# Backward attention loop: score and dP tiles cut into single PSUM banks, exp and product per head, dQ grouped by head and query-tile parity, and a new order of work inside a four-step block

## The chip, the cores and the metric

One Trainium2 chip, one of its cores. The metric is device time in microseconds (us) of one execution. The kernel before takes 1579.33 us (median of three runs, 1575.57 to 1579.68).

Engines: PE (matmuls), PEld (PE's weight loads), DVE (VectorE), ACT (ScalarE), POOL (GpSimd), SP (the engine that issues nearly all DMA here).

## The reference

A transformer block with attention and a gated feed-forward network in parallel, and all its gradients. S = 2048 tokens, D = 448, 16 heads of 28, F = 1792, bf16 in and out.

```python
def _A_ref(x, wqkv, wo):
    q, k, v = split_heads(x @ wqkv)                       # cut: reshape and transpose
    p = _softmax(jnp.einsum("bhqd,bhkd->bhqk", q, k) * (Dh ** -0.5), axis=-1)
    return merge_heads(jnp.einsum("bhqk,bhkd->bhqd", p, v)) @ wo

def _B_ref(x, w_gate, w_up, w_down):
    return (_silu(x @ w_gate) * (x @ w_up)) @ w_down

xn = _layernorm(x)
out = x + _A_ref(xn, wqkv, wo) + _B_ref(xn, w_gate, w_up, w_down)
# reference(...) returns out and, by jax.vjp, the gradients of x, wqkv, wo, w_gate, w_up, w_down
```

## The kernel before

The first 678 us are the forward pass and the parts of the backward pass that don't need attention's gradient. The last 57 us are a tail. Between them lies the backward attention loop, the only part that changes. It runs 512 **steps**; one step is one pair of heads, 128 queries and 512 keys. Four steps are a **block** (512 queries). In a step, PE recomputes the scores (S) of both heads, and dP for the step before. ACT takes exp(S). DVE multiplies dP by that exp, which gives dS. PE then multiplies exp and dS into the accumulators of dV and dK ("kv"). For dQ, dS has to be transposed: SP issues DMA transposes for most query tiles, and PE transposes the rest itself ("T", the `tr_unit`). Once per block PE computes dQ.

Between those, PE gets **fillers**: matmuls of other outputs, which use a PSUM bank called `genb`. They are y (the forward output), dx, dc, dwq (the gradient of wqkv), and "dsp", the transposes that dwq needs. 

A PSUM bank holds 512 fp32 per partition, and there are eight. (The Trainium skill, "PSUM — Partial Sum Buffer", "PSUM: the matmul accumulator" and "The four PSUM rules", says that there are 8 banks of 2 KiB and that one matmul's output lies in one; the allocation here agrees, since both kernels use exactly eight.) Before, they are: `sb` (scores) one tile of two banks, `db` (dP, and also the T tile) two tiles of two banks, `acc` one, `genb` one.

```python
def row(k):                                    # PE: S of step k, dP of step k-1
    if k < NB:
        ...
        s_ps = ps_b.tile([P, 2, 512], FP32, name="sb")             # two banks, one buffer
        for j in range(2):                                          # the two heads
            r = HP * (2 * hp + j)
            PE.matmul(s_ps[:, j, :], lhsT=qside[g, qc][r:r + HP, 0, qi * P:(qi + 1) * P],
                      rhs=kside[g, kc][r:r + HP, 0, :], start=True, stop=True, tile_position=(r, 0))
        sps[k] = s_ps
    if 1 <= k <= NB:
        d_ps = ps_b.tile([P, 2, 512], FP32, name="db", bufs=2)     # 2 x two banks
        ...                                                         # two matmuls, as above

def ew(k):                                     # ACT and DVE
    if k < NB:
        est[k] = bk.tile([P, 2, 512], BF16, name="e_sb", bufs=4)
        ACTE.activation(out=est[k][:], in_=sps.pop(k)[:], func=ACT.Exp, scale=SCALE)
    if 1 <= k <= NB:
        ...
        DVE.tensor_tensor(out=ds[:, qi % 2], in0=dps.pop(k - 1)[:], in1=est[k - 1][:], op=ALU.mult)
        ...                                                         # DMA transposes at qi 1 and 2

def tr_unit(b):                                # T: PE transposes of the last query tile(s)
    ...
    ps = ps_b.tile([P, 8 * (2 - q0), P], BF16, name="db", bufs=2)
    ...                                                             # 8 (16 for b < TB) PE.transpose
    DVE.tensor_copy(out=dsT[b][:, 2 + q0:4]..., in_=ps[:])

def kv(k):                                     # dV and dK, accumulated over 16 steps
    ...
    if last:
        ...
        ACTE.activation(out=dkv[g, hp][:, kc * 512:(kc + 1) * 512], in_=a[:], func=ACT.Copy, ...)

def dq_unit(b):
    ps = ps_b.tile([P, 512], FP32, name="genb")
    ...                                                             # 8 matmuls of 512 columns
    ACTE.mul(out=st[:], in_=ps[:], mul=SCALE)
    POOL.tensor_tensor(out=dq_acc[:, qsl], in0=dq_acc[:, qsl], in1=st[:], op=ALU.add)
    if kc == 3:
        POOL.dma_start(out=mv_[r0:r0 + 64, :], in_=dq_acc[64 - r0:128 - r0, qsl])
        ...                                                         # later: add the two halves

ROOM = {2: 600, 3: 400, 0: 1100}               # ns of filler after step 2, 3 and 0 of a block
for k in range(NB + 12):
    m = k % 4
    row(k); ew(k); ...
    while kv_n < NB and (kv_n <= k - 2 if m % 2 else kv_n <= k - 3 and blk < 1500):
        kv(kv_n); kv_n += 1
    ...                                        # m == 1: dq_unit; m == 2: tr_unit; 2, 3, 0: fill_step(m)
```

The softmax here doesn't subtract the row's maximum and nothing guards it: scores larger than these inputs give would overflow.

Of the kernel before, what the change touches and what calls it, by code (L numbers as in the profile page):

```python
# [16 lines left out]
S = 2048  # L17
# [73 lines left out]
def kernel(  # L91
# [610 lines left out]
    stream, later = [], []  # L702
# [14 lines left out]
    def row(k):  # L717

        if k < NB:
            g, hp, kc, qc, qi = steps[k]  # L720
            have(("q", g, qc), ("k", g, kc))
            s_ps = ps_b.tile([P, 2, 512], FP32, name="sb")
            for j in range(2):
                r = HP * (2 * hp + j)
                PE.matmul(s_ps[:, j, :], lhsT=qside[g, qc][r:r + HP, 0, qi * P:(qi + 1) * P],  # L725
                          rhs=kside[g, kc][r:r + HP, 0, :], start=True, stop=True, tile_position=(r, 0))
            sps[k] = s_ps
        if 1 <= k <= NB:
            g, hp, kc, qc, qi = steps[k - 1]
            d_ps = ps_b.tile([P, 2, 512], FP32, name="db", bufs=2)  # L730
            for j in range(2):
                r = HP * pv(2 * hp + j)
                PE.matmul(d_ps[:, j, :], lhsT=qside[g, qc][r:r + HP, 1, qi * P:(qi + 1) * P],  # L733
                          rhs=kside[g, kc][r:r + HP, 1, :], start=True, stop=True, tile_position=(r, 0))
            dps[k - 1] = d_ps

    def ew(k):
        if k < NB:
            est[k] = bk.tile([P, 2, 512], BF16, name="e_sb", bufs=4)
            ACTE.activation(out=est[k][:], in_=sps.pop(k)[:], func=ACT.Exp, scale=SCALE)  # L740
        if 1 <= k <= NB:
# [5 lines left out]
            DVE.tensor_tensor(out=ds[:, qi % 2], in0=dps.pop(k - 1)[:], in1=est[k - 1][:], op=ALU.mult)  # L747


# [8 lines left out]
    def tr_unit(b):  # L758
        ds = dss.pop(4 * b + 3)
        q0 = 1 if b >= TB else 0  # L760
        ps = ps_b.tile([P, 8 * (2 - q0), P], BF16, name="db", bufs=2)
        for c in range(8 * (2 - q0)):
            PE.transpose(ps[:, c, :], ds[:, q0 + c // 8, c // 4 % 2, (c % 4) * P:(c % 4 + 1) * P], ident_bf[:])  # L763
        DVE.tensor_copy(out=dsT[b][:, 2 + q0:4].rearrange("p q j kt s -> p (q j kt) s"), in_=ps[:])  # L764
# [35 lines left out]
    def dq_unit(b):  # L800

        while later:
            later.pop(0)()
# [4 lines left out]
        for kk in range(2):  # L808
            for par in range(2):
                for j in range(2):  # L810
                    r = HP * (2 * par + j)
                    h = HP * (2 * hp + j)
                    kt = 2 * kk + par
                    PE.matmul(ps[r:r + HP, :], lhsT=ks[:, kt, h:h + HP], rhs=t[:, :, j, kt, :],  # L814
                              start=(kk == 0), stop=(kk == 1), tile_position=(0, r), skip_group_check=True)
        qsl = slice(qc * 512, (qc + 1) * 512)
        if kc == 0:
            ACTE.mul(out=dq_acc[:, qsl], in_=ps[:], mul=SCALE)
            return
# [9 lines left out]
        ACTE.mul(out=st[:], in_=ps[:], mul=SCALE)  # L829
        POOL.tensor_tensor(out=dq_acc[:, qsl], in0=dq_acc[:, qsl], in1=st[:], op=ALU.add)  # L830
        if kc == 3:
            if hp == 0 and qc == 0:
                dqT[g] = bk.tile([P, S], BF16, name="dqT", bufs=1)
            r0 = 64 * hp
            mv_ = bk.tile([P, 512], FP32, name="dq_mv", bufs=1)
            POOL.dma_start(out=mv_[r0:r0 + 64, :], in_=dq_acc[64 - r0:128 - r0, qsl])

            def merge():
                POOL.tensor_tensor(out=dqT[g][r0:r0 + 64, qsl], in0=dq_acc[r0:r0 + 64, qsl],
                                   in1=mv_[r0:r0 + 64, :], op=ALU.add)  # L840
                if hp == 1 and g < G - 1:
                    store(dqkvT_d[3 * g, :, qsl], dqT[g][:, qsl])
                if hp == 1 and qc == 3 and g < G - 1:

                    stream[3:3] = [(480, lambda t8=t8: dsp_unit(g, 0, t8)) for t8 in range(2)]

                    at = [i for i, u in enumerate(stream) if u[1] in (dx_open, tail_open)]
                    at = max(at[0] + 1, 5) if g != 1 else 5
                    stream[at:at] = [(2590, lambda c=c: dwq_unit(g, c)) for c in range(4)]
            later.append(merge)  # L850
# [4 lines left out]
    def dsp_unit(g, kind, t8, tag="genb"):  # L855
        if g not in dsp:
            dsp[g] = bk.tile([P, NT, 3, P], BF16, name="dsp", bufs=1)
        src = dqT[g] if kind == 0 else dkv[g, kind - 1]
        ps = ps_b.tile([P, 8, P], BF16, name=tag, bufs=2 if tag == "rest" else 1)
        for j in range(8):  # L860
            t = 8 * t8 + j
            PE.transpose(ps[:, j, :], src[:, t * P:(t + 1) * P], ident_bf[:])
            if j < 7:
                yield 60
        DVE.tensor_copy(out=dsp[g][:, 8 * t8:8 * t8 + 8, kind, :], in_=ps[:])
        s_done.add((g, kind, t8))
        yield 60
# [3 lines left out]
    def dwq_unit(g, c, tag="genb"):  # L871
        d0, dn = DCH[c]
        ps = ps_b.tile([P, 3 * P], FP32, name=tag, bufs=2 if tag == "rest" else 1)
        for t in range(NT):
            PE.matmul(ps[:dn, :], lhsT=xn_sp[:, t, d0:d0 + dn], rhs=dsp[g][:, t].rearrange("p k r -> p (k r)"),  # L875
                      start=(t == 0), stop=(t == NT - 1))
            if t < NT - 1:
# [8 lines left out]
              o[:dn].rearrange("p k h r -> p k (h r)"))  # L886
        yield 162
# [66 lines left out]
    def dx_open():  # L954
        yst.close()
# [99 lines left out]
    ROOM = {2: 600, 3: 400, 0: 1100}  # L1055
    DRIP = 175 << 10
    cur, blk = None, 0

    def need(done):
        while not done():  # L1060
            for _ in stream.pop(0)[1]():
                pass

    def fill_step(m):
        nonlocal cur, blk
        room = ROOM[m]
        rest = sum(ROOM[x] for x in {2: (2, 3, 0), 3: (3, 0), 0: (0,)}[m]) + 150
        if cur is None:
            while stream and stream[0][0] == 0:
                for _ in stream.pop(0)[1]():  # L1070
                    pass
            if not stream or (m != 2 and stream[0][0] > rest):
                return
            ns, u = stream.pop(0)
            cur = u()
            blk += ns
        for ns in cur:
            room -= ns
            if room < ns / 2 and m != 0:
                return  # L1080
        cur = None

    kv_n = 0
    for k in range(NB + 12):
        now = k
        if k < NB:
# [5 lines left out]
            if hp == 1 and g + 1 < G and qi == 2 and (kc, qc) in ((1, 0), (3, 1), (3, 2), (3, 3)):  # L1092
# [8 lines left out]

        while kv_n < NB and (kv_n <= k - 2 if m % 2 else kv_n <= k - 3 and blk < 1500):
            kv(kv_n)
            kv_n += 1
        if m == 0 and 36 <= k < NB:
            fill_step(0)
        if m == 1:
# [3 lines left out]
        elif m == 2:  # L1111
            b = (k - 6) // 4
            if 0 <= b < NB // 4:
                tr_unit(b)
            blk = 0
            if 36 <= k < NB:
                fill_step(2)
        elif m == 3 and 36 <= k < NB:
            fill_step(3)
# [45 lines left out]
    def dx_b(t):  # L1165
# [7 lines left out]
        t2 = bk.tile([P, 512], FP32, name="e_sb", bufs=4)[:, :D]  # L1173
# [9 lines left out]
    def dsq_unit(t4, tag):  # L1183
# [9 lines left out]
    rest += [dsq_unit(t4, "rest") for t4 in range(4)]  # L1193
# [45 lines left out]
```

## Time and profile before

| window (us) | what | length |
|---|---|---|
| 0–678 | forward and early backward | 678 |
| 678–1516 | backward attention loop, 512 steps | 838 (1.636 a step) |
| 1516–1573 | tail | 57 |

Two stretches of the loop, from the windows view of the kernel before: busy time (and number of instructions) of each engine, then the granted PE clock, the DMA share and GB/s.

```profile
core 0: us, PE busy (x) PEld busy (x) DVE busy (x) ACT busy (x) POOL busy (x), PEclk, DMA share, GB/s
678.00:750.00 72.00, 48.80 (x505) 20.65 (x505) 55.15 (x48) 44.77 (x49) 3.80 (x3) 0.77 0.74 158
750.00:1516.00 766.00, 695.37 (x6899) 285.74 (x6895) 694.64 (x720) 563.31 (x655) 150.16 (x133) 0.99 1.00 196
```

PE and DVE are busy for 91% of the second stretch, ACT for 74%. The costliest groups of the loop (page, part 5: busy us and mean ns of one, then the idle time before them and what ended most of it):

```profile
L740 ACT ACTIVATE e_sb<-sb 128x1024 bf16<-128x1024 f32 x512 | 523.9, 1023 | 222.7 <-PE db L733 158.0
L747 DVE TENSOR_TENSOR ds_sb<-db,e_sb 128x1024 bf16<-128x1024 f32 x512 | 623.7, 1222 | 80.8 <-PE db L733 52.6
...
L764 DVE COPY dsT<-db 128x1024 bf16<-128x1024 bf16 (+1 forms) x128 | 91.5, 715 | 0.8 <-PE db L763 0.8
```

The timeline of ACT in the kernel before (start, length, what, and in brackets the idle time before it and its releaser):

```profile
1197.80 1.02 ACT L740 ACTIVATE e_sb<-sb 128x1024 bf16<-128x1024 f32 x1 [0.52 <-PE db L733]
1199.30 1.02 ACT L740 ACTIVATE e_sb<-sb 128x1024 bf16<-128x1024 f32 x1 [0.48 <-PE db L733]
1200.44 0.60 ACT L829 ACTIVATE dq_st<-genb 128x512 f32<-128x512 f32 x1
1200.93 1.02 ACT L740 ACTIVATE e_sb<-sb 128x1024 bf16<-128x1024 f32 x1
1202.43 1.02 ACT L740 ACTIVATE e_sb<-sb 128x1024 bf16<-128x1024 f32 x1 [0.48 <-PE sb L725]
```

Exps follow at 1.50 us although one takes 1.02: the only scores tile is free when an exp ends, and the next exp waits 0.48 us for new scores. The waits view shows the sum of this, and the waits of POOL for the small dQ transfer:

```profile
ACT e_sb L740 <- PE db L733: 158.0, 270, 5.5
...
POOL dqT L839 <- DMA dq_mv<-dq_acc: 94.8, 24, 8.0
...
ACT e_sb L740 <- PE sb L725: 62.5, 90, 17.8
```

### The profile page before, as it was taken

Reading aid. Unit: us, or ns where it says so; the run is one execution under the profiler, and the core shown is the slowest. Engines: PE = TensorE matmul, PEld = TensorE weight load, DVE = VectorE, ACT = ScalarE, POOL = GpSimd, SP = SyncE. Lnnn points to the kernel's source line nnn. Section 1 sums busy time; section 2 is a strip of 40 time slices with the busy share of each in tenths; the row PEclk is TensorE's granted clock in tenths of the full one; section 3 lists DMA queues with packets and bytes.
Section 4 is the critical chain, followed back from the end, with each engine's and each line's share of the span. In section 5 each row is a group of like instructions: output and inputs, shape, how many; then the busy total and the mean of one; then the engine's idle time right before and its main releaser. Section 6 shows DMA issues by size and latency. Waiting matters only on the chain. (4 is left out here: it accounts for less than half of the span.)

```text
span 1573.5 us, 30679 instructions
## 1 busy us (share of the span) xinstructions
PE 1356.6 (86%) x11728; PEld 550.4 (35%) x11728; DVE 1188.6 (76%) x1603; ACT 1148.8 (73%) x1320; POOL 434.3 (28%) x525
## 2 busy tenths in 40 slices
PE   5799889879989898847989979998899998998985
PEld 2333333323333333313333333433343333343332
DVE  6576666546666666348999989897989999989986
ACT  5588888768878888536777767776777777776753
POOL 3544433253444443000221211301312213110113
PEclk9899999989999999968999999999999999999998
DMA  4978856585767564359999998999989999999851
GB/s 122 197 186 186 201 115 145 149 178 142 165 158 182 138 159 113 80 144 184 217 206 216 214 209 155 199 226 210 222 167 169 197 213 221 172 187 195 161 125 49
DMA packets 687571, 270.38 MB, mean 172 GB/s; under 512 B 603952, under 2 KB 661824, under 8 KB 687424
## 3 DMA queue, kind: packets, MB, share of 16 engines
q1 hardware_dynamic: 681256, 259.14, 77.9%
q0 software_dynamic: 4592, 8.87, 2.6%
q8 instruction: 92, 1.51, 0.4%
q10 hardware_dynamic: 1576, 0.40, 0.1%
q14 instruction: 55, 0.45, 0.1%
HBM read 63.99 MB, written 58.85 MB: 78 GB/s over the span
## 5 line engine op out<-in xcount | busy, mean ns | idle before, releaser
L740 ACT ACTIVATE e_sb<-sb 128x1024 bf16<-128x1024 f32 x512 | 523.9, 1023 | 222.7 <-PE db L733 158.0
L747 DVE TENSOR_TENSOR ds_sb<-db,e_sb 128x1024 bf16<-128x1024 f32 x512 | 623.7, 1222 | 80.8 <-PE db L733 52.6
L558 ACT ACTIVATE eT<-s_ps 128x1024 bf16<-128x1024 f32 x512 | 492.0, 1025 | 115.4 <-PE s_ps L552 114.0
L830 POOL TENSOR_TENSOR dq_acc<-dq_acc,dq_st 128x512 f32<-128x512 f32 x88 | 111.2, 1264 | 596.8 <-ACT dq_st L829 517.7
L725 PE MATMUL sb<-kd,qd 32*128 32x512 bf16 x1024 | 203.6, 388 | 80.5 <-ACT e_sb L740 55.1
L733 PE MATMUL db<-kd,qd 32*128 32x512 bf16 x1024 | 202.6, 391 | 0.8 <-DVE ds_sb L747 0.5
L725 PEld LDWEIGHTS <-qd 32*128 32x128 bf16 x1024 | 76.0, 91 | 264.4 <-issue 236.5
L781 PE MATMUL acc<-ds_sb,qd 128*32 128x512 bf16 x1024 | 160.2, 393 | 0.9 <-DVE ds_sb L747 0.9
L777 PE MATMUL acc<-e_sb,qd 128*32 128x512 bf16 x1024 | 159.9, 393 | 0.0
L345 POOL TENSOR_TENSOR nn<-nn,ag 128x512 f32<-128x512 f32 x56 | 71.1, 1269 | 289.3 <-DVE ag L343 288.3
L552 PE MATMUL s_ps<-QQ,KK 32*128 32x512 bf16 x1024 | 112.3, 393 | 12.6 <-ACT eT L558 11.6
L985 PE MATMUL genb<-wguT,dau_c 128*128 128x448 bf16 x448 | 110.7, 357 | 5.2 <-DMA dau_c<-F_d 4.4
L384 PE MATMUL gen<-xn_t,f_sp 128*128 128x448 bf16 x448 | 97.4, 355 | 9.4 <-DVE nn L360 5.0
L763 PE MATMUL db<-ident_bf,ds_sb 128*128 128x128 bf16 x1088 | 84.5, 224 | 13.5 <-DVE ds_sb L747 5.8
L764 DVE COPY dsT<-db 128x1024 bf16<-128x1024 bf16 (+1 forms) x128 | 91.5, 715 | 0.8 <-PE db L763 0.8
L384 PEld LDWEIGHTS <-f_sp 128*128 128x128 bf16 x672 | 60.0, 98 | 91.5 <-issue 32.4
L763 PEld LDWEIGHTS <-ds_sb 128*128 128x128 bf16 x1088 | 71.1, 99 | 41.5 <-issue 35.8
L814 PE MATMUL genb<-dsT,kd 128*32 128x512 bf16 x1024 | 80.9, 390 | 1.8 <-DVE qd L825 1.2
L397 DVE CAST dw_o<-gen 128x448 bf16<-128x448 f32 x28 | 17.5, 625 | 79.8 <-PE gen L384 79.8
L367 PE MATMUL gen<-dyT,wT_f 128*128 128x512 bf16 x224 | 63.7, 389 | 15.0 <-DVE nn L360 14.9
L552 PEld LDWEIGHTS <-KK 32*128 32x128 bf16 x1024 | 28.2, 91 | 136.7 <-issue 135.7
L413 PE MATMUL gen<-eT,VS 128*32 128x512 bf16 x1024 | 69.6, 389 | 3.5 <-DVE nn L360 2.4
(159 smaller groups left out, 1845.7 us busy)
## 6 DMA issues: line engine op xcount, KB each, us to landing
F_d<-hda SPq DMA_DIRECT2D x56, 384.0 KB
dau_c<-F_d SPq DMA_DIRECT2D x56, 256.0 KB
qd<-QD_d SPq DMA_DIRECT2D x32, 256.0 KB
h_c<-F_d SPq DMA_DIRECT2D x24, 256.0 KB
dc<-dqkvT_d SPq DMA_DIRECT2D x12, 384.0 KB
kd<-KD_d SPq DMA_DIRECT2D x16, 256.0 KB
dsT<-ds_sb SPq DMA_TRANSPOSE x248
wT_d<-wT_f SPq DMA_DIRECT2D x14, 256.0 KB
```

Of the source, the lines that this page charges most:

```text
L384: PE.matmul(ps[:, :D], lhsT=fsp[fc][:, t // 4, w, t % 4, :], rhs=rhs[:, t, :], start=(t == 0), stop=(t == NT - 1))
L552: PE.matmul(s_ps[:, j, :], lhsT=KK[g][r:r + HP, kt * P:(kt + 1) * P], rhs=QQ[g][r:r + HP, qsl], start=True, stop=True, tile_position=(r, 0))
L558: ACTE.activation(out=eT[:], in_=sp2[hp][:], func=ACT.Exp, scale=SCALE)
L725: PE.matmul(s_ps[:, j, :], lhsT=qside[g, qc][r:r + HP, 0, qi * P:(qi + 1) * P], rhs=kside[g, kc][r:r + HP, 0, :], start=True, stop=True, t ...
L733: PE.matmul(d_ps[:, j, :], lhsT=qside[g, qc][r:r + HP, 1, qi * P:(qi + 1) * P], rhs=kside[g, kc][r:r + HP, 1, :], start=True, stop=True, t ...
L740: ACTE.activation(out=est[k][:], in_=sps.pop(k)[:], func=ACT.Exp, scale=SCALE)
L747: DVE.tensor_tensor(out=ds[:, qi % 2], in0=dps.pop(k - 1)[:], in1=est[k - 1][:], op=ALU.mult)
L763: PE.transpose(ps[:, c, :], ds[:, q0 + c // 8, c // 4 % 2, (c % 4) * P:(c % 4 + 1) * P], ident_bf[:])
L777: PE.matmul(a[r:r + HP, :], lhsT=sp4[:, 1, r:r + HP], rhs=e[:, j, :], start=first, stop=last, tile_position=(0, r), skip_group_check=True)
L781: PE.matmul(a[r:r + HP, :], lhsT=sp4[:, 0, r:r + HP], rhs=ds[:, qi % 2, j, :], start=first, stop=last, tile_position=(0, r), skip_group_ch ...
L830: POOL.tensor_tensor(out=dq_acc[:, qsl], in0=dq_acc[:, qsl], in1=st[:], op=ALU.add)
L985: PE.matmul(ps[:, :D], lhsT=d[:, i // 2, i % 2, tsl], rhs=dxs["w"][:, f0 + i // 2, i % 2, :], start=(i == 0), stop=(i == n - 1))
```

## The change

Its intent: take away the exp–scores–exp loop. The scores and dP become rings of three single banks each (3 + 3 + `acc` + `genb` = 8 again; a step needs two, so a ring holds one and a half steps), and exp and product work on one head at a time, so that PE can fill one bank while ACT reads another. ACT has room, so T's copy moves to it from DVE. dQ is grouped so that POOL needs no transfer between partitions. Filler time and the place of kv in the block are planned anew. T now works on one query tile per call.

```diff
-            s_ps = ps_b.tile([P, 2, 512], FP32, name="sb")
             for j in range(2):
+                s_ps = ps_b.tile([P, 512], FP32, name="sb", bufs=3)
...
-            d_ps = ps_b.tile([P, 2, 512], FP32, name="db", bufs=2)
             for j in range(2):
+                d_ps = ps_b.tile([P, 512], FP32, name="db", bufs=3)
...
-            est[k] = bk.tile([P, 2, 512], BF16, name="e_sb", bufs=4)
-            ACTE.activation(out=est[k][:], in_=sps.pop(k)[:], func=ACT.Exp, scale=SCALE)
+            est[k] = bk.tile([P, 2, 512], BF16, name="e_sb", bufs=5)
+            for j in range(2):
+                ACTE.activation(out=est[k][:, j], in_=sps.pop((k, j))[:], func=ACT.Exp, scale=SCALE)
...
-            DVE.tensor_tensor(out=ds[:, qi % 2], in0=dps.pop(k - 1)[:], in1=est[k - 1][:], op=ALU.mult)
+            for j in range(2):
+                DVE.tensor_tensor(out=ds[:, qi % 2, j], in0=dps.pop((k - 1, j))[:], in1=est[k - 1][:, j], op=ALU.mult)
...
-        ps = ps_b.tile([P, 8 * (2 - q0), P], BF16, name="db", bufs=2)
+        ps = ps_b.tile([P, 8, P], BF16, name="db", bufs=3)
...
-        DVE.tensor_copy(out=dsT[b][:, 2 + q0:4].rearrange("p q j kt s -> p (q j kt) s"), in_=ps[:])
+        ACTE.copy(out=dsT[b][:, q].rearrange("p j kt s -> p (j kt) s"), in_=ps[:])
...   (dq_unit, for three of the four head groups: 16 matmuls of 256 columns; the POOL transfer goes)
+            for kt in range(4):
+                for par in range(2):
+                    for j in range(2):
+                        PE.matmul(ps[r:r + HP, :256], lhsT=ks[:, kt, h:h + HP], rhs=t[:, par::2, j, kt, :], ...)
...
-            POOL.dma_start(out=mv_[r0:r0 + 64, :], in_=dq_acc[64 - r0:128 - r0, qsl])
...   (plan of a block)
-    ROOM = {2: 600, 3: 400, 0: 1100}
+    R2, R3, R0, BIG = 250, 750, 400, 10 ** 6
...
-        while kv_n < NB and (kv_n <= k - 2 if m % 2 else kv_n <= k - 3 and blk < 1500):
-            kv(kv_n)
-            kv_n += 1
+        if m:
+            while kv_n < NB and kv_n <= k - (2 if m == 2 or kv_n % 16 == 15 else 3) and (m != 2 or kv_n % 16):
+                kv(kv_n)
+                kv_n += 1
+        if m == 0:
+            ...
+            fill_step(R0)
+            ...
+                tr_unit(b, 3)
+            fill_step(BIG)
```

## The prediction

> **What bounds it now.** The windows view divides the span: forward to 678 us, backward loop 678 to 1516 us, tail 57 us. Only the loop changes: 512 steps, 1.636 us each (starts of the scores matmuls, timeline). In 750 to 1516 us PE is 91% busy, DVE 91%, ACT 74%. The timeline shows the limit: where one exp follows another directly, their starts are 1.50 us apart, at least 1.495. An exp takes 1.023 us (groups), its end frees the only two-bank scores tile, and the next exp starts 0.48 us later, after the scores matmul. This exp-scores-exp loop leaves ACT idle (before exps it waits 158 + 62 us for PE, waits view). The excess over 1.50 us is the step with tr_unit and filler (1.7 to 1.8 us) and the first 32 steps (1.83 us).
>
> **What the change does.** With three single banks, PE computes scores of one half while ACT works on another; the loop leaves the path, and throughput bounds. Costs per four-step block, by start-to-start times in the trace (neighbours overlap: the Trainium skill, "ScalarE: Activation LUTs", "What ACT_TABLE_LOAD costs", says about 93 ns for back-to-back ACTIVATEs; here 1.023 us exps of the forward start 0.90 to 0.92 us apart, which agrees):
> - ACT: eight half exps x 0.476 (a 512-wide step here) = 3.81, the transposed copy moved there 0.90, dQ scaling at 256 columns 0.26, other copies 0.24: 5.2 us.
> - DVE: eight half products x 0.60 = 4.8 (before 4 x 1.135), filler adds 0.5; the copy (0.62) goes: 5.3 us.
> - PE: scores with dP 0.86, dK/dV 0.86, dQ 0.43, transposes 0.44, filler 1.74, nine changes of tile shape x 0.097 (row to column tiles 0.314 against 0.216): 5.2 us; 5.9 with dwq.
> - SP: its DMA issues take 653 of these 766 us, 5.4 us a block; DMA share 0.92 to 1.09.
>
> The removed dq_mv transfers were off the path. So four queues meet at 5.2 to 5.4 us a block, 1.33 us a step, against 6.54. Perfect, that is 1.33 x 512 + 15 us for start and boundaries = 696 us for 836: about 1440 us. With rings of one and a half steps, queues within 5% of each other and dense DMA I add 5 to 8%.
>
> **Predicted: 1475 us**, 8 in 10 between 1440 and 1532. Faster 0.88, within 2% 0.10, slower 0.02.
>
> **What would show each step.** Right: half exps starting 0.48 us apart inside a step; ACT's waits before exps under 60 us; PE, DVE, ACT all about 90% busy in the loop; loop 720 to 740 us; forward and tail unchanged within 5 us; ACT busy up by about 230 us, DVE by about -10 us (0.16 x 512 - 91); half exps 0.60 us, half products 0.69 us; POOL's wait on dq_mv gone.
>
> Wrong: steps still 1.5 us apart (another loop holds: products freeing dP banks, or ACT's copy holding a dP bank); SP's transposes issuing in over 3.5 us and PE waiting on dau_c, dc or dsT (DMA holds); PE gaps growing since scores of two halves wait separately and no longer run as one 0.216 us group with dP.
>
> **What would make the prediction wrong.** DMA: uncontended packet times fill 0.74 of the 16 engines in the loop now, 0.86 to 0.9 after; if transposes slow beyond that, the loop stops near 1.5 us a step, the total near 1530. ACT's copy of transposed bf16 costing more than 0.9 us.

## The result, and the profile after

| | before | after |
|---|---|---|
| time, median (us) | 1577.45 (1574.92–1579.68, 4 runs) | 1559.16 (1556.25–1562.56, 4 runs) |
| loop (us: 512 mean steps), mean step | 838, 1.636 | 821, 1.603 |
| first 678 us, tail | 678, 57 | 677, 56 |

The ratio is 0.9885, with a 95% interval of 0.9857 to 0.9914: faster by 1.2%, so within 2%. A ratio here is the mean time of one kernel's runs over that of the other's of the same rounds, so it is not quite the ratio of the medians quoted. The predicted 1475 us and its range of 1440 to 1532 us missed.

The windows view of the kernel after, the same columns (the view stops at 1496, some 2 us before the loop's end):

```profile
678.00:750.00 72.00, 58.25 (x549) 21.03 (x546) 48.69 (x77) 58.04 (x104) 2.17 (x3) 0.76 0.68 162
750.00:1496.00 746.00, 696.23 (x7595) 283.04 (x7593) 652.61 (x1070) 662.87 (x1242) 70.32 (x85) 0.98 1.02 196
```

Groups (page, part 5) of the kernel after:

```profile
L749 DVE TENSOR_TENSOR ds_sb<-db,e_sb 128x512 bf16<-128x512 f32 x1024 | 648.8, 685 | 96.5 <-PE db L733 46.7
L741 ACT ACTIVATE e_sb<-sb 128x512 bf16<-128x512 f32 x1024 | 554.4, 613 | 84.9 <-PE db L733 59.5
...
L733 PE MATMUL db<-kd,qd 32*128 32x512 bf16 x1024 | 245.4, 390 | 18.7 <-DVE ds_sb L749 17.6
...
L763 ACT COPY dsT<-db 128x1024 bf16<-128x1024 bf16 x136 | 138.9, 1022 | 21.1 <-PE db L762 20.5
```

Waits view of the kernel after, whole span:

```profile
ACT e_sb L741 <- PE db L733: 59.5, 115, 6.5
...
ACT e_sb L741 <- PE sb L725: 18.6, 5, 17.6
PE db L733 <- DVE ds_sb L749: 17.6, 39, 2.7
```

ACT's idle time before exps fell from 222.7 to 84.9 us and POOL's wait is gone, as intended. A new wait is there: PE's dP matmul for DVE's product.

### Where PE's time goes

PE's busy share hides its waits. It rose from 91% to 93% in the long stretch, but a matmul record lasts 0.39 us while the next group can start 0.216 us after it, so a wait of up to 0.17 us does not show as idle at all. (The Trainium skill, "Perfetto Trace Analysis", "Identifying the Most-Contended Engine", says that matmul busy time is a poor measure of how near a kernel is to its limit, because matmuls are pipelined. This trace agrees, as the next table shows. The weight-load share, one of the two measures that the page offers in its place, reads 37% before and 38% after here, and the waits can't be read from it; the other, the share of peak arithmetic, was not worked out.)

So I worked the waits out from the trace's start times. The starts of two consecutive matmuls of known kinds (say dP, then a filler) are never closer than some least distance for that pair, for example 0.304 us; all that goes beyond it is counted as wait, if over 0.025 us. For blocks 0 to 126 (up to the start of the scores of the last block, hence a loop of 831 and 815 us instead of 838 and 821):

| blocks | before: n, us each, wait each, wait in all | after: n, us each, wait each, wait in all |
|---|---|---|
| first ten (no fillers yet; clock 0.77) | 10, 7.22, 3.68, **36.8** | 10, 7.38, 3.87, **38.7** |
| ordinary | 62, 6.23, 0.89, **55.2** | 60, 5.82, 0.49, **29.6** |
| with the dK/dV copy (every fourth) | 19, 6.49, 1.25, **23.7** | 19, 6.52, 1.34, **25.4** |
| with dsp transposes | 20, 6.55, 1.46, **29.1** | 20, 6.90, 1.90, **37.9** |
| with dwq | 13, 6.82, 0.67, **8.7** | 13, 6.55, 0.45, **5.8** |
| otherwise over 7.3 us | 3, 10.07, 4.39, **13.2** | 5, 9.11, 3.59, **18.0** |
| all | 127: loop 831.4, wait **166.7**, rest 664.7 | 127: loop 815.4, wait **155.6**, rest 659.8 |

PE's work is 660 to 665 us of the loop in either kernel (5.20 us a block after). The sums depend somewhat on how the least distances are chosen: worked out a second time from the same traces with another choice, the waits are 171 us before and 166 after, with the same order of classes. So the lengths of the blocks are firm, while a difference of some 10 us between two sums of waits is not. A second profile of the changed kernel shows what repeats: ordinary blocks 5.82 us again, dK/dV 6.46, but dsp 6.75, and the long blocks are in part others. The change moved the waits rather than removing them: by kind, before, the largest were scores waiting for the exp after a filler (52.6), T waiting behind dP (21.4) and dP behind scores (18.7); after, the second dP half behind the first (61.8), a filler behind dP (28.7) and the second scores half behind the first (22.7).

One ordinary block of the kernel after, timeline of PE, DVE and ACT. Each of the three is a view of its own.

```profile
870.92 0.61 PE L762 MATMUL db<-ident_bf,ds_sb 128*128 128x128 bf16 x8
871.46 0.39 PE L725 MATMUL sb<-kd,qd 32*128 32x512 bf16 x2
871.50 0.37 PE L733 MATMUL db<-kd,qd 32*128 32x512 bf16 x1
872.10 0.37 PE L733 MATMUL db<-kd,qd 32*128 32x512 bf16 x1 [0.23 <-DVE ds_sb L749]
872.40 0.39 PE L776 MATMUL acc<-e_sb,qd 128*32 128x512 bf16 x2
```

```profile
870.76 1.29 DVE L749 TENSOR_TENSOR ds_sb<-db,e_sb 128x512 bf16<-128x512 f32 x2 [0.29 <-PE db L733]
871.97 0.61 DVE L956 TENSOR_TENSOR yt<-genb,x_c 128x448 f32<-128x448 f32 x1
872.50 1.28 DVE L749 TENSOR_TENSOR ds_sb<-db,e_sb 128x512 bf16<-128x512 f32 x2
873.95 2.48 DVE L749 TENSOR_TENSOR ds_sb<-db,e_sb 128x512 bf16<-128x512 f32 x4 [0.17 <-ACT dq_st L836]
```

```profile
871.59 1.02 ACT L763 COPY dsT<-db 128x1024 bf16<-128x1024 bf16 x1
872.48 1.12 ACT L741 ACTIVATE e_sb<-sb 128x512 bf16<-128x512 f32 x2
```

T takes one of the three `db` banks at 870.92. The first dP half takes another at 871.50; the second must wait until 872.10, when DVE's second product of the step before has ended (870.76 + 1.29 = 872.05). The profile shows 0.23 us of idle time here; by start times the wait is 0.60. kv stands behind it in PE's queue and waits too. (The Trainium skill, "TensorE: Matmul & The Clock Gate", "Step-by-step: what each phase is for", says that PE pulls only weight loads ahead and keeps matmuls in program order; this place agrees: kv starts at 872.40, 0.30 us after the second dP half.) DVE meanwhile stands still for only 0.29 + 0.17 us: it is nearly full in this block, which is 5.66 us long.

In a block with dsp transposes something else waits. PE and DVE, kernel after:

```profile
1110.12 0.28 PE L877 MATMUL genb<-ident_bf,dkv 128*128 128x128 bf16 x2
1110.33 0.39 PE L725 MATMUL sb<-kd,qd 32*128 32x512 bf16 x2
1110.34 0.62 PE L733 MATMUL db<-kd,qd 32*128 32x512 bf16 x2
1111.78 0.55 PE L877 MATMUL genb<-ident_bf,dkv 128*128 128x128 bf16 x7 [0.82 <-DVE dsp L880]
```

```profile
1109.84 1.29 DVE L749 TENSOR_TENSOR ds_sb<-db,e_sb 128x512 bf16<-128x512 f32 x2 [0.42 <-ACT e_sb L741]
1111.05 0.68 DVE L880 COPY dsp<-genb 128x1024 bf16<-128x1024 bf16 x1
```

The single `genb` bank is full. The DVE copy that empties it is queued behind two products, and PE's next filler stands at the head of PE's queue and waits 0.82 us for it. The same wait of 0.89 us by start times comes back in ten of these twenty blocks. The change gives `genb` no second bank.

### The profile page after: what moved, and what is told of

The parts are those of the page before. It is cut to its first block, busy times and chain, and to the rows that moved or that the text cites. A ratio compares the mean times of both kernels' runs of the same rounds, so it can differ in the third digit from the quotient of the medians.

```text
span 1554.5 us, 33772 instructions
## 1 busy us (share of the span) xinstructions
PE 1366.3 (88%) x12496; PEld 547.8 (35%) x12496; DVE 1142.0 (73%) x1987; ACT 1265.1 (81%) x1968; POOL 352.8 (23%) x477
## 3 DMA queue, kind: packets, MB, share of 16 engines
q0 software_dynamic: 3440, 5.73, 1.8%
## 4 chain that ended last, share of the span: by engine, by line
PE 65%; DVE 16%; DMA 8%; ACT 5%; issue 4%; POOL 1%; SPq 0%; ACTq 0%; DVEq 0%; POOLq 0%
PE sb L725 9%; PE gen L384 8%; PE acc L776 7%; PE genb L1002 5%; PE s_ps L552 4%; PE genb L951 4%; PE db L762 3%; DMA dsT<-ds_sb 3%; DVE ds_sb L749 3%; PE db L733 3%; PE genb L820 3%; PE gen L329 2%; PE gen L413 2%; PE genb L890 2%; PE genb L1046 2%
## 5 line engine op out<-in xcount | busy, mean ns | idle before, releaser
L749 DVE TENSOR_TENSOR ds_sb<-db,e_sb 128x512 bf16<-128x512 f32 x1024 | 648.8, 685 | 96.5 <-PE db L733 46.7
L741 ACT ACTIVATE e_sb<-sb 128x512 bf16<-128x512 f32 x1024 | 554.4, 613 | 84.9 <-PE db L733 59.5
L733 PE MATMUL db<-kd,qd 32*128 32x512 bf16 x1024 | 245.4, 390 | 18.7 <-DVE ds_sb L749 17.6
L725 PE MATMUL sb<-kd,qd 32*128 32x512 bf16 x1024 | 217.2, 392 | 20.8 <-DMA qd<-QD_d 14.5
L838 POOL TENSOR_TENSOR dq_acc<-dq_acc,dq_st 128x256 f32<-128x256 f32 (+1 forms) x64 | 55.1, 861 | 629.4 <-ACT dq_st L836 550.7
L780 PE MATMUL acc<-ds_sb,qd 128*32 128x512 bf16 x1024 | 164.3, 398 | 0.0
L763 ACT COPY dsT<-db 128x1024 bf16<-128x1024 bf16 x136 | 138.9, 1022 | 21.1 <-PE db L762 20.5
L1002 PE MATMUL genb<-wguT,dau_c 128*128 128x448 bf16 x448 | 119.0, 357 | 10.7 <-DMA dau_c<-F_d 4.7
L725 PEld LDWEIGHTS <-qd 32*128 32x128 bf16 x1024 | 48.1, 91 | 167.7 <-issue 146.6
L384 PE MATMUL gen<-xn_t,f_sp 128*128 128x448 bf16 x448 | 97.5, 355 | 9.8 <-DVE nn L360 5.4
L346 POOL TENSOR_TENSOR nn<-nn,tt 128x512 f32<-128x512 f32 x56 | 71.0, 1268 | 4.4
```

The costliest lines, as they stand in the source:

```text
L384: PE.matmul(ps[:, :D], lhsT=fsp[fc][:, t // 4, w, t % 4, :], rhs=rhs[:, t, :], start=(t == 0), stop=(t == NT - 1))
L725: PE.matmul(s_ps[:], lhsT=qside[g, qc][r:r + HP, 0, qi * P:(qi + 1) * P], rhs=kside[g, kc][r:r + HP, 0, :], start=True, stop=True, tile_po ...
L733: PE.matmul(d_ps[:], lhsT=qside[g, qc][r:r + HP, 1, qi * P:(qi + 1) * P], rhs=kside[g, kc][r:r + HP, 1, :], start=True, stop=True, tile_po ...
L741: ACTE.activation(out=est[k][:, j], in_=sps.pop((k, j))[:], func=ACT.Exp, scale=SCALE)
L749: DVE.tensor_tensor(out=ds[:, qi % 2, j], in0=dps.pop((k - 1, j))[:], in1=est[k - 1][:, j], op=ALU.mult)
L763: ACTE.copy(out=dsT[b][:, q].rearrange("p j kt s -> p (j kt) s"), in_=ps[:])
```

## The experiments

Theories after the result:

- **Ring theory:** dP's ring (three banks, one lent to T) paces the loop in place of the scores' ring. Rings of one and a half steps are too short.
- **Throughput theory:** ACT and DVE, at 89% and 87% busy, are full, and no bank would help.
- **Transfer theory:** DMA, whose share was 1.00 before and is 1.02 after in the long stretch, delivers late.
- After the first batch of runs (exp_halves, d4s2, t_in_s, t_dve) a fourth stood beside them: **no one loop paces.** Several waits in different blocks add up, and taking one away lets the next show.

Sixteen further runs were made, of fourteen further kernels and two repeats. The ratios are to the kernel before, by runs on the same chip.

| kernel | median us | ratio to before (95%) | loop, blocks 0–126 | PE waits in it |
|---|---|---|---|---|
| changed kernel | 1559.16 | 0.9885 (0.9857–0.9914) | 815.4 | 155.6 |
| changed kernel again (five rounds) | 1555.87 | 0.9875 (0.9836–0.9913) | 812.9 | 153.8 |
| exp_halves | 1566.62 | 0.9923 (0.9900–0.9947) | 826.4 | 174.9 |
| dq_only | 1572.09 | 0.9947 (0.9918–0.9977) | 832.0 | 167.3 |
| old_plan | 1569.78 | 0.9930 (0.9899–0.9962) | 833.9 | 173.5 |
| d4s2 | 1594.41 | 1.0104 (1.0074–1.0133) | 853.7 | 188.2 |
| t_in_s | 1552.38 | 0.9821 (0.9789–0.9854) | 815.9 | 151.3 |
| t_dve | 1564.93 | 0.9921 (0.9893–0.9949) | 826.6 | 164.0 |
| dkv_late | 1555.97 | 0.9858 (0.9820–0.9896) | 816.6 | 157.2 |
| tb0 | 1561.59 | 0.9892 (0.9859–0.9925) | 822.4 | 165.2 |
| combo | 1559.59 | 0.9867 (0.9825–0.9910) | 818.8 | 159.7 |
| y_noload (wrong result) | 1545.15 | 0.9789 (0.9760–0.9818) | 802.7 | 143.8 |
| t_y4 | 1552.66 | 0.9830 (0.9791–0.9868) | 808.9 | 146.5 |
| t_y4_again (five rounds) | 1552.09 | 0.9839 (0.9809–0.9869) | 811.7 | 148.0 |
| x_free (wrong result) | 1539.69 | 0.9754 (0.9723–0.9784) | 796.3 | 128.3 |
| x_act (wrong result) | 1528.91 | 0.9689 (0.9657–0.9721) | 785.3 | 116.6 |
| x_act_dma (wrong result) | 1502.43 | 0.9533 (0.9499–0.9566) | 762.1 | 98.0 |

The loop and the waits come from one profiled execution each. Loop minus waits is 651 to 669 us in all of them. These runs hardly change PE's work, so this spread of 17 us also tells how far the last column can be trusted; small differences in it are not read here. The totals have a spread of their own: the forward part, which no run changes, takes 671 to 680 us in these profiles, and the profiled execution is one of four to six, not the median one (those of t_in_s, t_dve, tb0 and combo were the slowest of theirs).

### What each part of the change gives

**exp_halves**: on the kernel before, only the scores tile split into two single banks, with half exps.

```diff
-            s_ps = ps_b.tile([P, 2, 512], FP32, name="sb")
             for j in range(2):
+                s_ps = ps_b.tile([P, 512], FP32, name="sb", bufs=2)
...
-            ACTE.activation(out=est[k][:], in_=sps.pop(k)[:], func=ACT.Exp, scale=SCALE)
+            for j in range(2):
+                ACTE.activation(out=est[k][:, j], in_=sps.pop((k, j))[:], func=ACT.Exp, scale=SCALE)
```

> The kernel before with only the scores tile split into two single banks and the exp into two halves; dP, product, transposes, dQ and filler plan as before. If the exp-scores-exp loop of 1.50 us a step was the limit before, regular blocks fall from 6.18 to 5.7-5.9 us (DVE: 4 x 1.135 + 0.62 + 0.53 = 5.7), total 1535-1555 us, as much as the whole change. If another limit stood just behind it (dP tiles freed by products, the filler plan), blocks stay at 6.0-6.2 us and the total at 1565-1580 us.

Measured: 1566.62 us, 0.9923. The 1.50-us loop went in name, but PE's waits did not clearly fall (175 us against 167 by this working, while the loop got 5 us shorter): the second scores half now waits for the first half exp (67.8 us). Ordinary blocks stayed at 6.22 us; the gain came in the first ten blocks (72.2 to 66.7 us) and in dK/dV blocks. Halving alone does not open the loop. That the third bank is needed is seen in d4s2 below, which takes it away again.

**dq_only**: on the kernel before, only the dQ grouping with what hangs on it (no transfer, no merge, the new dsq_unit).

```diff
-            POOL.dma_start(out=mv_[r0:r0 + 64, :], in_=dq_acc[64 - r0:128 - r0, qsl])
-            ...                                   # and the merge
+        POOL.tensor_tensor(out=dqT[g][:, hp, qsl], in0=dq_acc[:, qsl], in1=st[:, :n], op=ALU.add)
...   (and the 16 matmuls of 256 columns, as in the change)
```

> The kernel before with only the dQ part of the change: groups by head and tile parity, no dq_mv transfer and no merge, a 256-column dQ copy; scores, dP, products, transposes and the filler plan as before. Since POOL and the dQ copy were off the path, I expect the total within 1% of before (1565-1585 us) and regular blocks at 6.18 us.

Measured: 1572.09 us, 0.9947; loop 832.0 us against 831.4, waits 167.3 against 166.7. In the trace the loop did not move at all. The timing is 0.5% lower, and its interval leaves out 1, so something small was gained; in the profiles the difference lies before the loop (first scores at 675.9 us against 678.5), which this edit does not touch. The removed transfer was off the critical path of the loop, as predicted.

**old_plan**: the changed kernel with the fillers, kv and T in the block as before.

```diff
-    R2, R3, R0, BIG = 250, 750, 400, 10 ** 6
+    ROOM = {2: 600, 3: 400, 0: 1100}
...
+        while kv_n < NB and (kv_n <= k - 2 if m % 2 else kv_n <= k - 3 and blk < 1500):
+            kv(kv_n)
+            kv_n += 1
```

> The changed kernel with the filler, dK/dV and transpose plan of the kernel before; rings of single banks, half exps and products, ACT's copy and the dQ part stay. If the rings alone bring the gain, the total is 1555-1565 us, as with the new plan. If a ring of one and a half steps needs work spread evenly over the four steps, the old plan, with up to 1.1 us of filler in one step and the transposes in another, makes PE wait more: 1570-1600 us.

Measured: 1569.78 us, 0.9930: no better than dq_only within the intervals. The rings without the plan give nothing beyond that: ordinary blocks are 6.27 us (before 6.23), dP's second half waits 52.8 us and T 33.6. The new plan without the rings was not tried. Rings and plan together are what brings ordinary blocks to 5.82.

### Which ring

**d4s2**: one bank moved from the scores to dP.

```diff
-                s_ps = ps_b.tile([P, 512], FP32, name="sb", bufs=3)
+                s_ps = ps_b.tile([P, 512], FP32, name="sb", bufs=2)
...
-                d_ps = ps_b.tile([P, 512], FP32, name="db", bufs=3)
+                d_ps = ps_b.tile([P, 512], FP32, name="db", bufs=4)
```

> The changed kernel with one PSUM bank moved from the scores ring to the dP ring (scores 2, dP 4). Ring theory: the dP ring, shared with the transposed tile, paces PE (second dP matmul of a step waits for a product, 62 us in the changed kernel's loop); then regular four-step blocks fall from 5.66 us to about 5.4 us, the dP-after-dP stall from 62 to under 30 us, and the total from 1559 to 1525-1545 us. Throughput theory (ACT and DVE are simply full at 5.66 us a block): regular blocks stay at 5.6-5.7 us, total within 5 us of 1559, or slower because the scores ring is only two deep.

Measured: 1594.41 us, 1.0104, slower than both kernels. dP's wait fell from 61.8 to 2.0 us and the scores' wait rose from 22.7 to 97.5. In the groups of d4s2 (page, part 5) the releaser of ACT's idle time has changed from dP to the scores:

```profile
L741 ACT ACTIVATE e_sb<-sb 128x512 bf16<-128x512 f32 x1024 | 559.6, 606 | 109.8 <-PE sb L725 64.8
L725 PE MATMUL sb<-kd,qd 32*128 32x512 bf16 x1024 | 286.5, 391 | 41.0 <-DMA qd<-QD_d 14.7
L733 PE MATMUL db<-kd,qd 32*128 32x512 bf16 x1024 | 206.7, 396 | 0.2 <-DVE ds_sb L749 0.2
```

(In the changed kernel dP's matmuls are busy for 245.4 us, here 206.7: two halves that run side by side cover less time than two that are pulled apart, so part of the wait sits inside the busy time.) The scores' ring needs its third bank, and there is no ninth to give dP a fourth. In this run alone PE could also reach dP later, since it is held up for the scores; but t_in_s, at the changed kernel's speed, and x_free lower the same wait (to 34.9 and 0.0 us), so the three together show the ring as the cause of dP's wait. That curing it makes a faster kernel is refuted for this cure.

**t_in_s**: T takes its bank from the scores' ring instead of dP's.

```diff
-        ps = ps_b.tile([P, 8, P], BF16, name="db", bufs=3)
+        ps = ps_b.tile([P, 8, P], BF16, name="sb", bufs=3)
```

> The changed kernel with three banks each, but the transposed tile taken from the scores ring instead of the dP ring. ACT frees both kinds there in its own order. Ring theory: the second dP matmul after a transpose no longer waits for the product one step earlier; regular blocks about 5.4 us, total 1525-1545 us, as with four dP banks. Throughput theory: 5.66 us and 1559 us unchanged.

Measured: 1552.38 us, 0.9821. dP's wait fell from 61.8 to 34.9 us, but the waits for `genb` (28.7 to 33.2), the scores (22.7 to 27.5) and others rose, and the sum went from 155.6 to 151.3 only. Ordinary blocks 5.83 us, as before this edit. The interval of t_in_s ends just below that of the changed kernel (0.9857) and overlaps that of its repeat (0.9836 to 0.9913), so a gain of its own is not clear.

**t_dve**: T's copy back on DVE.

```diff
-        ACTE.copy(out=dsT[b][:, q].rearrange("p j kt s -> p (j kt) s"), in_=ps[:])
+        DVE.tensor_copy(out=dsT[b][:, q].rearrange("p j kt s -> p (j kt) s"), in_=ps[:])
```

> The changed kernel with the copy of the transposed tile on DVE, as before, instead of ACT. DVE theory (DVE carries 5.34 us of 5.66 us a block): regular blocks rise to about 5.95-6.1 us, total 1580-1600 us, slower than before. ACT theory (extra ACT work such as the dK/dV copy adds in full, 0.65 us a block, because ACT is the limit): regular blocks fall below 5.6 us, blocks with the dK/dV copy below 6.0 us, and the total to 1530-1545 us.

Measured: 1564.93 us, 0.9921. ACT's idle time before exps rose from 84.9 to 170.1 us, DVE's before products fell from 96.5 to 51.1, and ordinary blocks went from 5.82 to 6.04 us. The blocks rose as the DVE theory said, the total by less (1580 to 1600 was expected). So in ordinary blocks DVE's load counts, and moving the copy to ACT was right, although ACT pays 1022 ns for what DVE does in 682.

### Repairs of single waits

**dkv_late**: in dK/dV blocks ACT's copy of the accumulator runs just before dQ's copy and keeps `genb` full. Here it runs after it.

```diff
         if last:
+            pend.append(lambda: evict(g, hp, kc, a))     # run after dq_unit of the next step m == 1
```

> The changed kernel, with ACT's copy of a finished dK/dV tile queued behind its copy of the dQ tile instead of ahead of it; no work added or removed. One-bank theory: the filler cannot start until ACT has emptied the only genb bank, and the dK/dV copy ahead of it (0.57 us) is waited for in full; then blocks with a dK/dV copy fall from 6.51 to 5.8-6.0 us, the wait of PE between dP and filler from 29 to 12-15 us in the loop, the total by 10-16 us (to 1543-1549 us). Full-ACT theory: the same work on ACT in another order costs the same, blocks stay at 6.5 us, total within 4 us of 1559.

Measured: 1555.97 us, 0.9858, no clear difference to the changed kernel. dK/dV blocks went from 6.52 to 6.68 us. ACT's order in the changed kernel:

```profile
1279.87 1.09 ACT L741 ACTIVATE e_sb<-sb 128x512 bf16<-128x512 f32 x2
1280.84 0.70 ACT L786 ACTIVATE dkv<-acc,cols 128x512 bf16<-128x512 f32 x1
1281.41 0.41 ACT L836 ACTIVATE dq_st<-genb 128x256 f32<-128x256 f32 x1
1281.67 2.10 ACT L741 ACTIVATE e_sb<-sb 128x512 bf16<-128x512 f32 x4
```

and what PE waits for in dkv_late, in the same sort of block:

```profile
1278.05 0.35 PE L1008 MATMUL genb<-wguT,dau_c 128*128 128x448 bf16 x1 [0.22 <-ACT dq_st L842]
1278.33 0.39 PE L725 MATMUL sb<-kd,qd 32*128 32x512 bf16 x1
1279.11 0.37 PE L725 MATMUL sb<-kd,qd 32*128 32x512 bf16 x1 [0.40 <-ACT e_sb L741]
```

In the changed kernel the filler waits 0.51 us for dQ's copy (PE's timeline, kernel after):

```profile
1281.87 0.35 PE L1002 MATMUL genb<-wguT,dau_c 128*128 128x448 bf16 x1 [0.51 <-ACT dq_st L836]
```

In dkv_late that is 0.22, but the exps now stand behind both copies and the scores' second half waits 0.40 by the profile. ACT must do both copies in front of four half exps, and either order makes one ring wait.

**tb0**: the first eight blocks used two PE transposes each, with two copies on ACT; here one, as all other blocks.

```diff
-    TB = 8
+    TB = 0
```

> The changed kernel with one transpose a block on PE and one copy on ACT from the start, not two in the first eight blocks (the DMA makes the other). If ACT's two copies (0.9 us each) hold the start, the first ten blocks fall from 73.8 us to 64-69 us and the total by 5-9 us. If start is held by loads (queries and keys arriving) or by slow PE clock, 73-75 us and total unchanged.

Measured: 1561.59 us, 0.9892, the same as the changed kernel. The first ten blocks took 71.8 us against 73.8, not the 64 to 69 expected, and the rest of the loop took this back (13 blocks over 7.3 us among all after the tenth, against 10).

**combo**: t_in_s, dkv_late, TB = 0 and four buffers for y at once (`bufs=4` as in t_y4 below).

> The changed kernel with four repairs: transposed tile in the scores ring, dK/dV copy behind the dQ copy, four store buffers for the forward output, and one transpose a block from the start. If the losses are separate and local, as I think, their gains add: 7 (measured, transposed tile) + 13 + 4 + 6 us, total 1525-1538 us. If they only move waits elsewhere, 1545-1555 us.

Measured: 1559.59 us, 0.9867. The first ten blocks gained 7.7 us (66.1), the rest of the loop lost 11 (752.7 against 741.6). The repairs don't add. This fits the fourth theory, but doesn't prove it: much of the loss lies in long blocks, which differ from run to run (14 over 7.3 us here after the tenth, 10 in the changed kernel, 8 in its repeat), and the profiled execution was a slow one.

### Transfers

In several long blocks a y unit waits for a transfer. Waits view of the kernel after, in the window of block 26 (9.62 us long):

```profile
DVE y L959 <- DMA out_dram<-y: 2.9, 1, 2.9
PEld L820 <- issue: 2.7, 1, 2.7
PE genb L820 <- DVE y L959: 2.4, 1, 2.4
```

DVE must write y into one of two buffers whose store has not finished; `genb` stays full for it, and dQ waits.

**y_noload**: the later y chunks reuse the data of the first instead of loading their own. The output y is wrong, and only that one.

```diff
+        if ch:
+            ych[ch, half] = ych[0, half]
+            ych[ch, 2 + half] = ych[0, 2 + half]
+            return
```

> The changed kernel with a wrong output on purpose: the forward output's filler uses the activations of the first chunk for all four, so six loads of about 0.45 MB between 700 and 900 us are not made; all else, matmuls too, is as it was. DMA theory: the irregular blocks of that stretch (7.4 to 9.6 us, blocks 23, 26, 30, 33, 36 to 38, some 20 us over the regular ones) come from DMA transposes landing late while these loads are in flight; then at least half of that excess goes, total 1543-1550 us. Rival: they come from dependences between the engines (banks, fillers); then the same blocks stay long and the total stays within 4 us of 1559.

Measured: 1545.15 us, 0.9789, some 14 us under the changed kernel. (The expectation understates the edit: by the DMA views 8.45 MB are not moved, six loads of some 1.4 MB.) Two ordinary blocks over 7.3 us were left of five; the means of all other classes stayed (ordinary 5.78, dK/dV 6.48, dsp 6.85). So these loads cost some 1% here, in single blocks. They don't set the pace of the ordinary ones: the transfer theory holds in part. The edit takes away SP's issuing of the loads as well as the bytes, and the run can't tell the two apart.

Block by block, the seven that the expectation names took 44.3 us before the change, 58.7 in the changed kernel (50.1 in its repeat) and 42.1 here, while blocks 55, 70, 97 and 113 took 38.5 us here against 29.0. So these blocks became long with the change, and not by the loads alone: before, the same stretch (750 to 940 us) had a DMA share of 1.09 and two blocks over 7.3 us (34 and 35), where the changed kernel has a share of 1.06 and seven. Long waits also went with a lower clock: in this stretch the granted clock was 0.99 before, 0.94 in the changed kernel and 0.99 in y_noload, and after the wait of 2.45 us at 854 us two kv groups start 0.39 us apart instead of 0.216.

**t_y4**, and **t_y4_again** with five rounds: t_in_s with four y buffers instead of two.

```diff
-            y = yp.tile([P, D], BF16, name="y")
+            y = yp.tile([P, D], BF16, name="y", bufs=4)
```

> The changed kernel with the transposed tile in the scores ring (1552 us measured) and four store buffers for the forward output instead of two: block 26 (9.85 us, product of y waits for an older store) falls to about 5.9 us, total 1545-1551 us, the best correct kernel so far.

> The transposed tile in the scores ring and four store buffers for the forward output: ratio to before 0.980-0.985, 4 to 9 us below the changed kernel in the same rounds. If the earlier difference was between chips, the two are within 3 us.

Measured: 1552.66 us (0.9830), and again 1552.09 us (0.9839, 0.9809 to 0.9869). Block 26 took 5.86 us as expected, but it did so in the repeat of the changed kernel too, with two buffers, so this shows nothing of the buffers; and the total missed its 1545 to 1551. By median it is level with t_in_s (1552.38), whose ratio is the lowest of the correct kernels (0.9821). It does beat the kernel before (by 1.6%). Whether it beats the changed kernel stays unclear; the changed kernel ran beside it again:

> The changed kernel itself, on the same chip and in the same rounds as t_y4_again: ratio to before 0.986-0.991.

Measured: 1555.87 us, 0.9875 (0.9836 to 0.9913). The intervals overlap.

### Taking away several waits at once

These three give wrong gradients. Each does as much PE work as the changed kernel.

**x_free**: the product reads exp twice instead of dP and exp. dP is still computed, and nobody reads it, so its banks never wait for DVE.

```diff
-                DVE.tensor_tensor(out=ds[:, qi % 2, j], in0=dps.pop((k - 1, j))[:], in1=est[k - 1][:, j], op=ALU.mult)
+                dps.pop((k - 1, j))
+                DVE.tensor_tensor(out=ds[:, qi % 2, j], in0=est[k - 1][:, j], in1=est[k - 1][:, j], op=ALU.mult)
```

> The changed kernel with wrong gradients on purpose: the product reads the exp tile twice (bf16, SBUF) and leaves the dP banks unread, so PE never waits for a dP bank to be freed by a product and DVE's work falls by about half; all matmuls, exps, copies and transfers stay. If the wait moved to the dP ring and to DVE is where the gain went, the dP-after-dP stall (62 us) goes to under 5 us, regular blocks fall to PE's own 5.2-5.4 us and the total by 30-60 us, to 1500-1530 us. If ACT or DMA hold the loop just as closely, the waits appear at the scores ring or the transposes instead and the total stays above 1545 us.

Measured: 1539.69 us, 0.9754: 19 us less. The product is cheaper as well, so the run cannot tell the ring from DVE's load; it takes both away. Groups (page, part 5) of x_free:

```profile
L750 DVE TENSOR_TENSOR ds_sb<-e_sb 128x512 bf16<-128x512 bf16 x1024 | 418.0, 442 | 211.7 <-ACT e_sb L741 120.9
...
L733 PE MATMUL db<-kd,qd 32*128 32x512 bf16 x1024 | 202.6, 392 | 0.0
```

dP's wait is zero, and DVE's busy time over the span fell from 1142.0 to 917.0 us. Yet 128 us of PE waits are left. Ordinary blocks fell only from 5.82 to 5.70; dK/dV (6.43) and dsp blocks (6.87) hardly moved. The ring theory and the throughput theory for DVE together explain at most 20 us of the time, and 27 us of the waits.

**x_act**: x_free, and T's copy and the dK/dV copy on DVE, which now has room.

```diff
-        ACTE.copy(out=dsT[b][:, q]..., in_=ps[:])
+        DVE.tensor_copy(out=dsT[b][:, q]..., in_=ps[:])
...
-            ACTE.activation(out=dkv[g, hp][:, kc * 512:(kc + 1) * 512], in_=a[:], func=ACT.Copy, scale=...)
+            DVE.tensor_scalar(out=dkv[g, hp][:, kc * 512:(kc + 1) * 512], in0=a[:], scalar1=..., scalar2=None, op0=ALU.mult)
```

> Wrong gradients on purpose, as x_free, and ACT's copies of the transposed tile and of dK/dV moved to DVE, which now has room. ACT's work falls from 5.2 to about 4.1 us a block, DVE's is about 4.0, PE's stays 5.2. If ACT was the next limit: blocks with a dK/dV copy fall from 6.3 to 5.3-5.7 us, light blocks from 5.41 to 4.8-5.0 us, the loop from 796 to 740-765 us, the total from 1540 to 1485-1512 us. If the plan on PE or DMA holds the rest, blocks stay at 5.4 and 6.3 us and the total above 1530 us.

Measured: 1528.91 us, 0.9689: another 11 us. The first ten blocks fell from 65.1 to 56.4 us and dK/dV blocks from 6.43 to 6.09. Ordinary blocks stayed (5.73). So ACT's extra copies cost at the start and in dK/dV blocks, not in ordinary ones.

**x_act_dma**: x_act and the edit of y_noload.

> As x_act, and the forward output's loads of chunks 2 to 4 not made (out_0 wrong too). If the limits lie one behind another and DMA is the last of them, another 10-25 us go, total 1470-1495 us, near the 1475 us predicted, and what is left over PE's 680 us of work in the loop is the start, the wait for loads at the group boundary and the genb bank. If DMA transposes are slow everywhere, less than 8 us go.

Measured: 1502.43 us, 0.9533: another 26 us, against 14 for the same edit on the changed kernel. This time ordinary blocks fell too (5.73 to 5.57 us), and dsp blocks from 6.87 to 6.45, so with the other waits gone the loads count in more than single blocks. Here the windows view of x_act_dma shows ACT and DVE far from full (78% and 76%) and PE at 94%:

```profile
690.00:1440.00 750.00, 702.79 (x8072) 298.32 (x8071) 567.67 (x1297) 586.62 (x1165) 77.92 (x88) 0.99 1.03 197
```

and still 98 us of PE waits: 20.0 in the first ten blocks, 28.3 in dsp blocks, 17.8 in four long ones, 14.8 in dK/dV blocks, 12.6 in all 61 ordinary ones.

## Why the prediction was wrong

Point by point:

- **The exp–scores–exp loop bounds the steps, and three banks remove it.** Right for the ordinary blocks with rings and plan together: 6.23 to 5.82 us on average (light ones 5.66). Half exps start 0.476 to 0.493 us apart inside a step in five of six steps (predicted 0.48).
- **Durations.** Half exps 613 ns on average (predicted 600), half products 685 ns (690), ACT's copy 1022 ns and 0.89 start to start (0.90). Right.
- **PE 5.2 us a block.** Right for the sum: 659.8 us over 127 blocks is 5.20; 1.33 × 512 was 681. By class it agrees partly by luck: 5.33 in ordinary blocks and 6.10 with dwq (predicted 5.9), made up for by 3.51 in the first ten, which have no fillers.
- **ACT idle before exps below 60 us by the two waits.** Missed a little: 59.5 + 18.6 = 78. ACT busy +230 us was wrong: +116, mostly because busy time counts overlapping neighbours once and half exps overlap (554.4 us for 1024 of 613 ns; dQ's copies also got shorter, 71.7 to 53.0 us in all); DVE −10 was −47, by the same effect in the half products (648.8 us for 1024 of 685 ns). The sums by start-to-start times in the prediction were not hurt by that.
- **The removed dq_mv transfers are off the path.** Right (dq_only: loop 832.0 against 831.4).
- **Forward and tail unchanged, POOL's wait gone.** Right.
- **Transposes slowing SP.** Did not happen: the median time to issue one of two query tiles was 3.04 us before and 2.96 after. The DMA risk came true in another form, single blocks that wait for stores and loads.
- **Loop 720 to 740 us.** Wrong: 821.

The step that failed is the sum "1.33 x 512 + 15 us for start and boundaries = 696 us for 836", with "I add 5 to 8%" for the waits. It is a term of the sum that was mis-sized, the waits: 15 us for start and boundaries, and 35 us from the 5% that led to 1475, make 50 us beside the 681 of 1.33 x 512. The loop took 821, so 140 us beside the 681; PE's waits, worked out from the trace, are 155.6 us (PE's work came out below 681). The error behind it was the step "the loop leaves the path, and throughput bounds", taken for the mean block of 6.54 us, as if nothing else held any block once the exp loop was gone. In the kernel before, only 55 of 167 us of PE waits lay in ordinary blocks. The change nearly halved these: 29.6 are left, 9% on top of PE's work in these blocks, close to the 5 to 8%. But 103 us lay in the first ten blocks, in dK/dV blocks, in dsp blocks and in a few long ones (36.8 + 23.7 + 29.1 + 13.2), and there the change gained nothing: 120 us after (38.7 + 25.4 + 37.9 + 18.0). In dK/dV and dsp blocks a filler's end to the next scores was the largest wait before (14.7 of 23.7 and 12.8 of 29.1 us), so the exp loop was last there too (and in part in the first ten, where by the waits view up to 750 us PE's scores waited 17.9 us for exps before and 6.1 after). It is gone after, and waits for `genb` (11.9 and 14.4 us) and dP (9.1 and 14.7 us) have taken its place.

That other causes stand behind it in those blocks is shown by runs for some: ACT's extra copies at the start and in dK/dV blocks (x_act: −8.7 us in the first ten blocks, −0.34 us per dK/dV block), and y's loads for long blocks (y_noload: −14 us, which also takes their issuing off SP). For dsp blocks the single `genb` bank behind DVE's queue is read from the timeline, and no run took it away, since no ninth bank is to be had. One run agrees in part: in x_free, with shorter products ahead of the copy in DVE's queue, the wait of 0.89 us falls to some 0.5 us in blocks 49, 65 and 81, and these blocks from 6.5 to 6.8 us to 5.9; other dsp blocks got longer there, so the mean stayed.

Of the theories, the ring theory is right about dP's wait (d4s2) and wrong about what it is worth. The throughput theory is right for DVE in ordinary blocks (t_dve: +0.22 us) and is not the bound elsewhere, since x_act_dma has three engines at 76 to 94% by the windows view and still 98 us of waits. What stays, as I read it from these runs: PE's queue is in order, each ring reaches no further than one and a half steps, and what delays ACT or DVE once in a block is often paid by PE. No run shows this as a whole.

Open: the 98 us left in x_act_dma. One of its long blocks, block 58, takes 11.4 to 13.1 us in every kernel but d4s2 (7.43), the kernel before included; by the trace it waits for the loads of dx's operand, which no run tested. The first ten blocks wait in part at a granted clock of 0.76 to 0.77, which both kernels have. Also open is how the 19 us of x_free divide between the ring and DVE's load.

## What to carry to other kernels

A loop that paces a step is worth what it costs in the blocks where it is the last wait, so sort the steps by what else they carry and price each class by itself; the mean step mixes them. Matmul busy time can read 91% while PE waits for a fifth of the loop: count waits by the start times of matmuls. Count for every PSUM ring what must happen on which in-order queue between a bank's last use and its next, and look for the next-shortest ring to show as soon as the first is mended, as the scores' ring did in d4s2.

## What the Trainium skill lacked or had wrong

- "TensorEngine Tiling (Array Packing)", "Key Properties", says that a change of tiling mode drains PE, but gives no time. Here it costs some 0.1 us: a kv group (128x32 tiles) starts at least 0.300 to 0.315 us after dP (32x128 tiles), where groups of the same shape follow at 0.216.
- "ScalarE: Activation LUTs", "What ACT_TABLE_LOAD costs", gives an overlap of about 93 ns for back-to-back ACTIVATEs. For half exps it was somewhat more: 592 to 603 ns each, 0.476 to 0.494 us apart, some 0.10 to 0.12 us of overlap.
- "DMA: Bandwidth & Descriptors", "DMA Transpose (X-bar)", gives no time for SP to issue a transpose, and no page gives one for the size used here. In the kernel before, one of two query tiles took 1.7 to 4.7 us of SP's queue (median 3.0), one of a single tile 1.2 to 2.6 (median 1.3), and all together 509 of the 766 us from 750 to 1516.
- "Perfetto Trace Analysis", "Identifying the Most-Contended Engine", offers the weight-load share, beside the share of peak arithmetic, in place of matmul busy time. The weight-load share stayed at 37 to 38% here while PE waited 155 to 167 us, and from it alone the waits can't be read; matmul start times were what showed them.
